# A three-layer fp32 kernel on one core: a later operand load, a second pair of split buffers, and a thinner schedule for unpacking weights

## Chip, cores and metric

One core of a Trainium2 chip. The metric is device microseconds (us) of one execution of the whole program, the median of several runs. Of the core's engines, TensorE (PE in the profile) does the matrix products, VectorE (DVE), ScalarE (ACT) and GpSimd (POOL) work element by element, and SyncE (SP) issues the DMAs, in order.

## What is computed

Windowed attention (two kinds of mask), then a mixture layer over 8 experts with weights `P` from a Sinkhorn loop, then a plain two-matrix layer with a squared ReLU:

```python
x = attention(q, k, v).reshape(2304, 512)
P = sinkhorn(x @ w_gate)                       # 2304 x 8
out = sum(P[:, e:e+1] * (relu(x @ w1[e]) @ w2[e]) for e in range(8))   # 512 -> 1024 -> 512
out = square(relu(out @ w_in)) @ w_out          # 512 -> 2048 -> 512
```

All of it is fp32. The last layer's weights `w_in` and `w_out` come as 64-bit numbers, which the kernel itself narrows to fp32.

## The kernel before

**Phases and steps.** After the attention the program runs 80 steps, in four phases: steps 0 to 31 and 32 to 63 are the expert layer for two sets of 1024 tokens ("pairs" of 512), steps 64 to 71 and 72 to 79 the last layer for the same two sets; `first` holds 0, 32, 64, 72. The remaining 256 tokens (the "single") go along in steps 0 to 31 and 64 to 71. One step handles 256 hidden features: a first product (units u1 to u7, a Strassen-like scheme of seven block products with matrices `blk` and `sum`), and the second product of the step before (l2 units, or v1 to v7 in the "mixed" phases 32 to 63 and 72 to 79). Each unit is mostly six 128x512 matmuls, since each fp32 operand is split into a high and a low part and three products are added. A step of the phase 32 to 63 has 14 units, one of the phase 64 to 71 has 18.

**What sets the order.** The order is written out: each engine's instructions stand in program order. `run(u)` issues a unit and then whatever `after(k, f)` put down k units later, so place k is the k-th unit of a step and what is past its end falls into the next step. Each engine runs its own list in order and waits only on semaphores, so that an instruction that waits holds up all behind it on its engine.

**What the change touches.**

- Splitting a weight or an operand into two parts is a cast on ACT (high) and a subtraction on DVE (low). `prep_w(i)` (L150) places the weight splits of a step; for steps 64 to 70 line 239 gives the places of `w2` high and low, the two POOL groups m3 and m4 (L229 to L234), and the "mix" high and low (L252). The last one's `mix_done` (L248) then issues the next load of `raw2` (L144) and the stores of the mix.
- `narrow` (L261) turns 64-bit weights into fp32 in 32 pieces of four stages: a load into `xb` (L266), two DVE stages of two instructions (L273 and L277; L281 and L284), and a last DVE stage of three (L288, L291, L295) with a store (L296). `narrow_on` (L1092) runs one stage, at places that `stages` (L1168 to L1172) gives: in steps 2 to 29 four a step, and in steps 52 to 60 two a step.
- `blocks_of(c, ...)` (L300) splits the seven blocks of a phase's activations, in halves j, for phase c + 1: a cast into `hi` (L307), a subtraction into `lo` (L310), stores of both to `b_dram` (L312), and a POOL subtraction for the next block (L303). There is one pair `hi`, `lo`. For c = 2 the pair is the two halves of `mixh0`, and `split_on(2, ...)` (L1162 to L1164) puts two splits in each of steps 66 to 69 and five in step 70, at places 2, 5, 8, 12 and 16.
- `operands_single` (L894) loads the single's activations from `y_dram` into an `xb` tile (L896) and splits them into `xs` (L339 on ACT, L340 on DVE), for use from step 64 on; it is called in step 60 (L1165).

`xb` tiles are two rotating buffers of 128x1024: a new tile gets the buffer of the tile before the last.

In u5, `after(0, ...)` copies the PSUM bank `pt` to SBUF (L717 on ACT), and only then may u6 write that bank; L713 is the same behind u4 and L701 behind u1. In the mixed phases v1 is copied from two banks to two others (L866 on ACT) before v2 adds to them; the same copies are behind casts (L646) whose input a POOL chain (L678) makes from the DVE product L667 (`mix<-s,pp`).

Of the kernel before, what the change touches and what calls it, by code (L numbers as in the profile page):

```python
# [1 line left out]

# [8 lines left out]
F32R = mybir.dt.float32r  # L11
# [24 lines left out]
NS1 = E * SPE  # L36
# [3 lines left out]
PAIRS = (0, 1280)  # L40
# [7 lines left out]
def tile_kernel(ctx: ExitStack, tc: tile.TileContext, a):  # L48
# [12 lines left out]
    at = att.enter_context(tc.tile_pool(name="at", bufs=2))  # L61
# [20 lines left out]
    y_dram = dram.tile([128, KC, NTOK], F32, name="y_dram")  # L82
# [13 lines left out]
    def tmp(name):  # L96
        return post[0].tile([128, 512], F32, tag="tmp", name=name, bufs=3)
# [8 lines left out]
    mixes = []  # L106
# [7 lines left out]
    def kept(i):  # L114
        return NS1 <= i < 2 * NS1 or i >= first[3]

    def mixed(i):
        return kept(i) and i < len(steps) - 1

    def place(i):  # L120
        return i % NS1 if i < first[2] else NS1 + (i - first[2]) % NS2

    def store(n, s, w):
        for h, z in zip("hl", w):
            nc.sync.dma_start(w_dram[n + h][s], z.bitcast(F32))

    def fetch(n, i, w):
        for h, z in zip("hl", w):
            nc.sync.dma_start(z.bitcast(F32), w_dram[n + h][place(i)])
# [7 lines left out]
    def load_w(i, which):  # L137
        if i >= len(steps) or kept(i):
            return
        moe, s = steps[i]  # L140
        while not moe and done[0] < 16 * s + 8 * which + 8:
            narrow_on()
        dst = raw1.rearrange("p b c -> p (b c)") if which == 0 else raw2
        nc.sync.dma_start(dst, src_w(i, which))  # L144
# [5 lines left out]
    def prep_w(i):  # L150
# [6 lines left out]
        def hi(w, src):  # L157
            return lambda: nc.scalar.copy(w[0], src)

        def lo(w, src, then=lambda: None):  # L160
            def f():
                nc.vector.tensor_tensor(out=w[1], in0=src, in1=w[0].bitcast(F32), op=ALU.subtract)  # L162
                then()

            return f

        n = i + 1
        late = 4 if i == 2 * NS1 else 0
# [3 lines left out]
        elif n < len(steps):  # L172
# [23 lines left out]
            at = (4, 5, 6, 8) if n == NS1 else (2, 3, 4, 5) if n == 1 else (2, 5, 10, 14) if n < NS1 else (2, 5, 8, 11)  # L196
            spread = n > first[2] + 1
            if spread:
                at = (6, 7, 14, 16)
# [6 lines left out]
        if kept(i):  # L206
            w2 = wset[i % 2]["w2"]
            out += [(0, lambda: fetch("w2", i, w2))]
            if mixed(i):
                out += [(0, lambda: fetch("mix", i, mixes[i % 2]))]  # L210
            if i == 2 * NS1 - 3:
                out += [(2, lambda: load_w(2 * NS1 + 1, 0)), (2, lambda: load_w(2 * NS1, 1))]
        elif i >= 0:
            w2 = wset[i % 2]["w2"]
            moe = i < NS1
            r = raw2.rearrange("p (f e d) -> p f e d", f=FC, e=2)
            z = mix32.rearrange("p (k d) -> p k d", k=4)

            def m1():
                tt(out=c(z, 0), in0=r[:, 0, 1], in1=r[:, 1, 1], op=ALU.add)  # L220
                tt(out=c(z, 2), in0=r[:, 0, 0], in1=r[:, 0, 1], op=ALU.subtract)

            def m2():
                tt(out=c(z, 1), in0=c(z, 0), in1=r[:, 0, 0], op=ALU.subtract)
                tt(out=c(z, 3), in0=r[:, 1, 0], in1=c(z, 1), op=ALU.subtract)
                load_w(i + 1, 1)

            def m3():
                tt(out=r[:, 1, 1], in0=r[:, 0, 1], in1=r[:, 1, 1], op=ALU.add)  # L229
                tt(out=r[:, 0, 1], in0=r[:, 0, 0], in1=r[:, 0, 1], op=ALU.subtract)  # L230

            def m4():
                tt(out=r[:, 0, 0], in0=r[:, 1, 1], in1=r[:, 0, 0], op=ALU.subtract)
                tt(out=r[:, 1, 0], in0=r[:, 1, 0], in1=r[:, 0, 0], op=ALU.subtract)  # L234

            if moe:
                at = (0, 0, 0, 1, 9, 10) if i == 0 else (1, 3, 6, 7, 13, 15)
            else:
                at = (11, 13, 14, 14, 16, 17) if late else (12, 13, 14, 14, 19, 20)
            if i:  # L240
                out += [(at[0], hi(w2, raw2)), (at[1], lo(w2, raw2, lambda: store("w2", place(i), w2)))]
            if moe:
                out += [(at[2], m1), (at[3], m2)]
                out += [(at[4], hi(mixes[1], mix32)), (at[5], lo(mixes[1], mix32, lambda: store("mix", place(i), mixes[1])))]
            elif i + 1 < first[3]:
                m = mixes[1]

                def mix_done():  # L248
                    load_w(i + 1, 1)
                    store("mix", place(i), m)  # L250

                out += [(at[2], m3), (at[3], m4), (at[4], hi(m, raw2)), (at[5], lo(m, raw2, mix_done))]  # L252
        else:
            w2 = wset[0]["w2"]
            out += [(6, hi(w2, raw2)), (7, lo(w2, raw2, lambda: kept_back.append(lambda: store("w2", 0, w2))))]
        return out

    def xb():
        return post[0].tile([128, 2 * T], F32, tag="xb", name="xb", bufs=2)
# [39 lines left out]

    def blocks_of(c, src, spaces):  # L300

        z11, z12, z21, z22, hi, lo = spaces
        sub = lambda o, x, y: nc.gpsimd.tensor_tensor(out=o, in0=x, in1=y, op=ALU.subtract)  # L303

        def block_of(k, j, z, then=lambda: None):
            def cast():
                nc.scalar.copy(hi, z)  # L307

            def rest():
                nc.vector.tensor_tensor(out=lo, in0=z, in1=hi.bitcast(F32), op=ALU.subtract)  # L310
                for h, y in enumerate((hi, lo)):
                    nc.sync.dma_start(b_dram[c][k, h, :, j], y.bitcast(F32))  # L312
                then()

            return cast, rest

        for j in range(2):
            def load(j=j):
                for h, zs in enumerate(((z11, z12), (z21, z22))):
                    for t, z in enumerate(zs):  # L320
                        nc.sync.dma_start(z, src[:, 2 * h + j, t * T:t * T + T])

            yield load, lambda: None
            yield block_of(0, j, z11, lambda: sub(z11, z12, z11))
            yield block_of(1, j, z21, lambda: sub(z12, z22, z12))
            yield block_of(4, j, z11, lambda: sub(z11, z22, z11))
            yield block_of(6, j, z12)
            yield block_of(2, j, z22, lambda: sub(z21, z21, z11))
            yield block_of(5, j, z11)
            yield block_of(3, j, z21)  # L330
# [217 lines left out]
    first = [0, NS1, 2 * NS1, 2 * NS1 + NS2]  # L548
# [24 lines left out]
    def after(k, f):  # L573

        due.setdefault(clock[0] + k, []).append(f)
# [318 lines left out]
    def operands_single():  # L894
        z = xb().rearrange("p (k n) -> p k n", n=NSG)
        nc.sync.dma_start(z, y_dram[:, :, SINGLE:SINGLE + NSG])  # L896
        return single_pieces(z)
# [3 lines left out]
    with tc.manual_schedule():  # L901
# [89 lines left out]
        def slot(i):  # L991
# [33 lines left out]
            (NG + LAG - 2, (f() for f in single_pieces(xf[:, :, SINGLE:SINGLE + NSG]))),  # L1025
        ]
        prep0 = [f for _, f in prep_w(-1)]
        for i in range(NG + LAG):
            slot(i)
# [27 lines left out]
        for g in gates:  # L1057
            for _ in g:
# [14 lines left out]
        two = lambda z: (z[:, :512], z[:, 512:])  # L1073
        held = [post[0].tile([128, T], F32, tag="pp", name="pp", bufs=3) for _ in range(3)]
        splits = [
            blocks_of(
                0, x_dram,
                (tmp("z11"), tmp("z12"), tmp("z21"), held[0], held[1].bitcast(F32R), held[2].bitcast(F32R)),
            ),
        ]  # L1080

        def split_on(c, k, k_lo):
            cast, rest = next(splits[c], (None, None))
            if cast:
                after(k, cast)
                after(k_lo, rest)
# [14 lines left out]
        for i in range(len(steps) + 1):  # L1101
# [52 lines left out]
                splits.append(blocks_of(1, y_dram[:, :, :2 * T], y0 + raw))  # L1154
            if i == 2 * NS1 + 1:
                y1 = two(mix32) + tuple(post[0].tile([128, T], F32, tag="pp", name="pp", bufs=3) for _ in range(2))
                splits.append(blocks_of(2, y_dram[:, :, PAIRS[1]:], y1 + two(mixes[0][0])))
            if SCALED <= i < NS1 - 2:
                split_on(0, 8, 9)
            elif NS1 + 4 <= i < 2 * NS1 - 4:  # L1160
# [1 line left out]
            elif 2 * NS1 < i < 2 * NS1 + 7:  # L1162
                for k in {2 * NS1 + 1: (3, 8, 16), 2 * NS1 + 6: (2, 5, 8, 12, 16)}.get(i, (3, 16)):
                    split_on(2, k, k + 1)  # L1164
            if i == first[2] - 4:  # L1165
                for k, f in enumerate(operands_single()):
                    after(8 + 2 * k, f)
            stages = {}  # L1168
            if SCALED - 1 <= i < NS1 - 2:
                stages = {2: 0, 16: 1, 17: 2, 1: 3}  # L1170
            elif 2 * NS1 - 12 <= i <= 2 * NS1 - 4:
                stages = {7: 1, 10: 2} if i % 2 else {7: 3, 8: 0}  # L1172
            for k, u in enumerate(order):
                run(u)
                if i < SCALED:
# [87 lines left out]
```

## Time and profile before

| | |
|---|---|
| median of 3 runs | 1961.62 us (1958.82 to 1964.09) |
| the profiled execution, its own time | 1961.02 us |
| its span, first to last instruction | 1959.2 us |
| mean granted TensorE clock | 0.994 |
| DMA moved | 491.84 MB, mean 251 GB/s |

"Busy" is the time in which an engine executes instructions. Matmuls overlap in the records, so the progress of PE is read from the starts of its matmuls. In rows of a timeline the bracket at the end is the idle time of the engine just before the row and what ended it; "PEclk" is the granted share of the full clock.

### The profile page before, as it was taken

The numbers are of one execution on the slowest core, as the hardware profiler recorded it, in microseconds if no ns is written. First come the engines' busy times: TensorE is split into PE (matmuls) and PEld (weight loads), VectorE is DVE, ScalarE is ACT, GpSimd is POOL, SyncE is SP. The second block draws the span as 40 slices with busy tenths as digits, with TensorE's granted clock in tenths as the row PEclk, the third lists the DMA queues.
The fourth block names the chain that finished last, engine by engine and source line by source line (L and its number), as shares of the span: only waits on it lengthen the run. The fifth ranks groups of instructions, "written<-read, shape, count | busy, mean of one in ns | idle before, by whom it ended". The sixth has DMA issues, their size and how long they took to land.

```text
span 1959.2 us, 29443 instructions
## 1 busy us (share of the span) xinstructions
PE 1926.5 (98%) x11050; PEld 1601.8 (82%) x11050; DVE 1630.2 (83%) x2337; ACT 747.3 (38%) x1238; POOL 633.5 (32%) x556
## 2 busy tenths in 40 slices
PE   8999999999999999999999999999998999999999
PEld 6778888888888888888888888888877878878887
DVE  5868888888888888887489998998998887775897
ACT  3544433333333332333333434333333354443443
POOL 4632333223333332222133424333232233330331
PEclk9999999999999999999999999999999999999999
DMA  7665667667666566666957758666575876669661
GB/s 261 217 239 197 253 262 269 259 257 265 236 251 234 229 241 247 230 232 263 395 216 273 285 215 297 252 252 249 225 260 193 311 293 252 251 241 392 232 253 67
DMA packets 166399, 491.84 MB, mean 251 GB/s; under 512 B 17248, under 2 KB 40176, under 8 KB 166256
## 3 DMA queue, kind: packets, MB, share of 16 engines
q1 hardware_dynamic: 166256, 489.96, 66.6%
q8 instruction: 87, 1.43, 0.3%
q14 instruction: 56, 0.46, 0.1%
HBM read 281.15 MB, written 208.74 MB: 250 GB/s over the span
## 4 chain that ended last, share of the span: by engine, by line
PE 89%; DVE 6%; DMA 1%; ACT 1%; POOL 1%; issue 1%; ACTq 0%; POOLq 0%; DVEq 0%
PE mm L779 28%; PE pt L566 15%; PE s L566 10%; PE xt L566 10%; PE mm L862 9%; PE mm L750 6%; PE s L862 3%; PE xt L862 3%; DVE acc L876 2%; PE xt L439 1%; DVE g L649 1%; PE mm L972 1%; PE s L387 1%; POOL r L678 1%; DMA sg<-w_mixl 1%
## 5 line engine op out<-in xcount | busy, mean ns | idle before, releaser
L779 PE MATMUL mm<-w2h,g 128*128 128x512 f32 x1312 | 406.5, 391 | 0.0
L801 DVE SCALAR_TENSOR_TENSOR acc<-mm,ptile,acc 128x512 f32<-128x512 f32 x290 | 216.7, 748 | 103.8 <-PE mm L779 103.5
L779 PEld LDWEIGHTS mm<-w2h,g 128*128 128x128 f32 x1312 | 245.5, 188 | 50.2
L779 PE MATMUL mm<-w2l,g 128*128 128x512 f32 x656 | 255.8, 390 | 0.0
L678 POOL TENSOR_TENSOR r<-mix,r 128x512 f32<-128x512 f32 x39 | 51.2, 1314 | 556.1 <-DVE mix L667 399.0
L649 DVE TENSOR_TENSOR g<-r,g 128x512 fp32r<-128x512 f32 x156 | 159.4, 1022 | 46.9 <-ACT g L646 45.2
L176 POOL TENSOR_TENSOR sums<-raw 128x256 f32<-128x256 f32 x40 | 32.7, 817 | 489.6 <-DVE suml L162 441.1
L646 ACT CAST g<-r 128x512 fp32r<-128x512 f32 x156 | 96.8, 621 | 137.4 <-PE mm L862 99.1
L779 PEld LDWEIGHTS mm<-w2l,g 128*128 128x128 f32 x656 | 123.4, 188 | 25.9
L876 DVE TENSOR_TENSOR acc<-mm,acc 128x512 f32<-128x512 f32 x226 | 144.6, 680 | 0.0
L566 PE MATMUL pt<-x_hi,sumh 128*128 128x512 f32 x320 | 124.9, 390 | 2.0 <-ACT s L713 2.0
L566 PE MATMUL s<-x_hi,blkh 128*128 128x512 f32 x320 | 125.4, 392 | 1.1 <-ACT pt L701 1.1
L566 PE MATMUL xt<-x_hi,sumh 128*128 128x512 f32 x320 | 124.7, 390 | 0.0
L566 PE MATMUL s<-x_lo,blkh 128*128 128x512 f32 x320 | 124.7, 390 | 0.0
L566 PE MATMUL s<-x_hi,blkl 128*128 128x512 f32 x320 | 124.6, 389 | 0.0
L566 PE MATMUL pt<-x_hi,suml 128*128 128x512 f32 x320 | 124.6, 389 | 0.0
L566 PE MATMUL xt<-x_hi,suml 128*128 128x512 f32 x320 | 124.5, 389 | 0.0
L566 PE MATMUL pt<-x_lo,sumh 128*128 128x512 f32 x320 | 124.5, 389 | 0.0
L566 PE MATMUL xt<-x_lo,sumh 128*128 128x512 f32 x320 | 124.5, 389 | 0.0
L604 ACT ACTIVATE sg<-mm 128x512 fp32r<-128x512 f32 (+1 forms) x35 | 19.7, 563 | 272.8 <-PE mm L750 272.8
L750 PE MATMUL mm<-xs,blkh 128*128 128x256 f32 x640 | 115.8, 280 | 0.0
L604 ACT ACTIVATE g<-s 128x512 fp32r<-128x512 f32 x96 | 59.6, 621 | 136.5 <-DVE s L718 69.0
(220 smaller groups left out, 4809.8 us busy)
## 6 DMA issues: line engine op xcount, KB each, us to landing
raw<-in_w SPq DMA_DIRECT2D x61, 512.0 KB, 6.5
blkh<-w_blkh SPq DMA_DIRECT2D x41, 512.0 KB, 3.6
blkl<-w_blkl SPq DMA_DIRECT2D x41, 512.0 KB, 4.4
sumh<-w_sumh SPq DMA_DIRECT2D x41, 512.0 KB, 5.3
suml<-w_suml SPq DMA_DIRECT2D x41, 512.0 KB, 6.1
w_blkh<-blkh SPq DMA_DIRECT2D x40, 512.0 KB, 6.1
w_blkl<-blkl SPq DMA_DIRECT2D x40, 512.0 KB, 6.5
w_sumh<-sumh SPq DMA_DIRECT2D x40, 512.0 KB, 6.3
```

The source lines that it names most:

```text
L176: tt(out=c(sums, 0), in0=c(raw1, 2), in1=c(raw1, 3), op=ALU.add)
L387: nc.tensor.matmul(ps[QB * head:QB * head + QB, 2 * (g % 3) + g // 3, :], qt[rows, pr, g * QB:g * QB + QB], kt[rows, pr, g * QB:g * QB + K ...
L566: nc.tensor.matmul(ps, w[:, c], z[:, x, j], start=start and k == 0, stop=stop and k == 5, skip_group_check=True)
L604: after(k, lambda: nc.scalar.activation(out=ghi, in_=src, func=AF.Relu))
L646: after(k, lambda: nc.scalar.copy(b[:, 0], src))
L649: lambda: nc.vector.tensor_tensor(out=b[:, 1], in0=src, in1=b[:, 0].bitcast(F32), op=ALU.subtract),
L678: sub = lambda o, x, y: nc.gpsimd.tensor_tensor(out=o, in0=x, in1=y, op=ALU.subtract)
L750: nc.tensor.matmul(ps[:, n * NSG:n * NSG + NSG], w[:, c], z[:, kc], start=k == 0, stop=k == 3 * KC - 1)
L779: nc.tensor.matmul(ps, g[:, c0 * 128:c0 * 128 + 128], wt[:, fc], start=k == 0, stop=k == 3 * FC - 1)
L801: nc.vector.scalar_tensor_tensor(out=dst, in0=ps, scalar=p, in1=dst, op0=ALU.mult, op1=ALU.add)
L862: nc.tensor.matmul(ps, w[wt][:, c], z[:, g], start=start and k == 0, stop=stop and k == 2, skip_group_check=True)
L876: nc.vector.tensor_tensor(out=o, in0=ps, in1=o, op=ALU.add)
```

## The change

It touches four places. In `prep_w` the mix split of step 64 moves from places 16 and 17 to 20 and 22, and in step 65 all six places move back by two. `blocks_of` takes any number of `hi`, `lo` pairs and uses them in turn; for c = 2 a second pair, the two halves of an `xb` tile taken in step 65, is added. `operands_single` is called in step 62 rather than 60. One more piece is narrowed in step 30 (load at place 2, stages at places 12, 13 and 14); the three pieces that are left run in steps 52 to 61, one stage a step, with the load of the next piece behind the last stage.

```diff
@@ -1,3 +1,4 @@
+import itertools
 from contextlib import ExitStack
 
 import numpy as np
@@ -236,7 +237,7 @@
             if moe:
                 at = (0, 0, 0, 1, 9, 10) if i == 0 else (1, 3, 6, 7, 13, 15)
             else:
-                at = (11, 13, 14, 14, 16, 17) if late else (12, 13, 14, 14, 19, 20)
+                at = (11, 13, 14, 14, 20, 22) if late else (14, 15, 16, 16, 21, 22) if n == first[2] + 2 else (12, 13, 14, 14, 19, 20)
             if i:
                 out += [(at[0], hi(w2, raw2)), (at[1], lo(w2, raw2, lambda: store("w2", place(i), w2)))]
             if moe:
@@ -299,10 +300,13 @@
 
     def blocks_of(c, src, spaces):
 
-        z11, z12, z21, z22, hi, lo = spaces
+        z11, z12, z21, z22 = spaces[:4]
+        pairs = itertools.cycle(zip(spaces[4::2], spaces[5::2]))
         sub = lambda o, x, y: nc.gpsimd.tensor_tensor(out=o, in0=x, in1=y, op=ALU.subtract)
 
         def block_of(k, j, z, then=lambda: None):
+            hi, lo = next(pairs)
+
             def cast():
                 nc.scalar.copy(hi, z)
 
@@ -1154,7 +1158,7 @@
                 splits.append(blocks_of(1, y_dram[:, :, :2 * T], y0 + raw))
             if i == 2 * NS1 + 1:
                 y1 = two(mix32) + tuple(post[0].tile([128, T], F32, tag="pp", name="pp", bufs=3) for _ in range(2))
-                splits.append(blocks_of(2, y_dram[:, :, PAIRS[1]:], y1 + two(mixes[0][0])))
+                splits.append(blocks_of(2, y_dram[:, :, PAIRS[1]:], y1 + two(mixes[0][0]) + two(xb().bitcast(F32R))))
             if SCALED <= i < NS1 - 2:
                 split_on(0, 8, 9)
             elif NS1 + 4 <= i < 2 * NS1 - 4:
@@ -1162,14 +1166,16 @@
             elif 2 * NS1 < i < 2 * NS1 + 7:
                 for k in {2 * NS1 + 1: (3, 8, 16), 2 * NS1 + 6: (2, 5, 8, 12, 16)}.get(i, (3, 16)):
                     split_on(2, k, k + 1)
-            if i == first[2] - 4:
+            if i == first[2] - 2:
                 for k, f in enumerate(operands_single()):
                     after(8 + 2 * k, f)
             stages = {}
             if SCALED - 1 <= i < NS1 - 2:
                 stages = {2: 0, 16: 1, 17: 2, 1: 3}
-            elif 2 * NS1 - 12 <= i <= 2 * NS1 - 4:
-                stages = {7: 1, 10: 2} if i % 2 else {7: 3, 8: 0}
+            elif i == NS1 - 2:
+                stages = {2: 0, 12: 1, 13: 2, 14: 3}
+            elif 2 * NS1 - 12 <= i <= 2 * NS1 - 3:
+                stages = ({8: 3, 9: 0}, {8: 1}, {8: 2})[(i - 2 * NS1 + 12) % 3]
             for k, u in enumerate(order):
                 run(u)
                 if i < SCALED:
```

The order of PE's instructions and of POOL's is the same in both kernels. The line numbers of the changed kernel are higher: by one up to `prep_w`, by four from the blocks' splits on.

**ACT, steps 60 and 62.** Rows of step 60, from the copy behind u4 to the first operands of the next unit; `xs<-xb` is the cast of the single's operands. Before:

```order
L713 COPY s_12973<-pt 128x512
L339 CAST xs<-xb 128x1024
L717 COPY s_12974<-pt 128x512
L646 CAST g_2263<-r_9039 128x512
L646 CAST g_2263<-mix_2266 128x512
```

Of the change, the same place in step 62:

```order
L717 COPY s_13249<-pt 128x512
L343 CAST xs<-xb 128x1024
L721 COPY s_13250<-pt 128x512
L650 CAST g_2263<-r_9050 128x512
L650 CAST g_2263<-mix_2266 128x512
```

In the change step 60 has the two copies next to each other, and the cast stands two steps later between the same two copies (L713 and L717 are L717 and L721 there).

**ACT, beginning of step 65.** `mixh<-raw` is the high half of step 64's mix, `s<-pt` the copies behind u4 and u5. Before:

```order
L701 COPY pt<-s 128x512
L158 CAST mixh_2268<-raw_109 128x1024
L611 ACTIVATE r<-s_13586 128x512
L611 ACTIVATE r<-s 128x512
L621 CAST g_2263<-g 128x512
L713 COPY s_13707<-pt 128x512
L621 CAST g_2264<-g 128x512
L717 COPY s_13708<-pt 128x512
```

Of the change:

```order
L705 COPY pt<-s 128x512
L615 ACTIVATE r<-s_13586 128x512
L615 ACTIVATE r<-s 128x512
L625 CAST g_2263<-g 128x512
L717 COPY s_13707<-pt 128x512
L625 CAST g_2264<-g 128x512
L159 CAST mixh_2268<-raw_109 128x1024
L721 COPY s_13708<-pt 128x512
```

The cast went from behind the copy of u1 to just ahead of the copy of u5; on DVE the low half moved with it, from ahead of the two products `g<-s,r` to behind the addition after u5.

**ACT, step 70.** The casts of blocks for c = 2 around the copies of u4 and u5. Before:

```order
L307 CAST mixh_2267<-mix_2266 128x512
L611 ACTIVATE r<-s 128x512
L713 COPY s_14825<-pt 128x512
L621 CAST g_2263<-g 128x512
L307 CAST mixh_2267<-mix_2266 128x512
L717 COPY s_14826<-pt 128x512
```

Of the change:

```order
L311 CAST xb<-mix_2266 128x512
L615 ACTIVATE r<-s 128x512
L717 COPY s_14826<-pt 128x512
L625 CAST g_2263<-g 128x512
L311 CAST mixh_2267<-mix_2266 128x512
L721 COPY s_14827<-pt 128x512
```

Nothing changed its place; successive casts write different pairs.

## Rows read from the trace of the kernel before

**Rows 1.** The page's busy time by engine (us, share of the span, instructions).

```profile
PE 1926.5 (98%) x11050; PEld 1601.8 (82%) x11050; DVE 1630.2 (83%) x2337; ACT 747.3 (38%) x1238; POOL 633.5 (32%) x556
```

**Rows 2.** Waits of PE over the span (total us, times, longest).

```profile
PE pt L566 <- ACT s L717: 10.1, 3, 6.0
```

**Rows 3.** Stretches: us; PE, PEld, DVE, ACT, POOL busy; PEclk; DMA share; GB/s.

```profile
880.00:920.00 40.00, 40.00 (x201) 34.09 (x200) 31.54 (x38) 12.92 (x19) 14.60 (x16) 1.00 0.61 228
1366.00:1492.00 126.00, 124.25 (x541) 100.64 (x540) 117.07 (x182) 45.80 (x80) 41.89 (x28) 1.00 0.59 218
1480.00:1520.00 40.00, 33.56 (x139) 26.99 (x138) 31.85 (x48) 13.64 (x23) 11.97 (x8) 0.91 0.55 211
1720.00:1760.00 40.00, 36.31 (x173) 30.53 (x172) 27.42 (x39) 16.41 (x26) 16.05 (x15) 0.91 0.63 238
1760.00:1800.00 40.00, 40.00 (x189) 33.62 (x188) 23.13 (x35) 10.88 (x18) 0.00 (x0) 1.00 1.01 393
```

**Rows 4.** Timeline of PE, steps 60, 65 and 70 (start, duration, instruction).

```profile
1497.07 0.39 PE L862 MATMUL xt<-g,mixl 128*128 128x512 f32 x1
1503.46 0.80 PE L566 MATMUL pt<-x_hi,blkh 128*128 128x512 f32 x1 [6.00 <-ACT s L717]
...
1508.16 0.39 PE L566 MATMUL xt<-x_hi,sumh 128*128 128x512 f32 x1
...
1601.20 0.50 PE L566 MATMUL pt<-x_hi,sumh 128*128 128x512 f32 x1 [1.48 <-ACT s L713]
...
1737.81 0.80 PE L566 MATMUL pt<-x_hi,blkh 128*128 128x512 f32 x1 [3.69 <-ACT s L717]
...
1743.05 0.39 PE L566 MATMUL xt<-x_hi,sumh 128*128 128x512 f32 x1
```

**Rows 5.** Timeline of ACT, steps 60, 65 and 70.

```profile
1501.88 1.04 ACT L339 CAST xs<-xb 128x1024 fp32r<-128x1024 f32 x1 [7.87 <-DMA xb<-y_dram]
...
1595.96 1.05 ACT L158 CAST mixh<-raw 128x1024 fp32r<-128x1024 f32 x1 [0.68 <-POOL raw L234]
...
1736.66 0.62 ACT L307 CAST mixh<-mix 128x512 fp32r<-128x512 f32 x1 [5.41 <-DMA b_dram<-mixh]
```

**Rows 6.** What SP waited for, steps 60 and 61.

```profile
SPq L896 <- DVE xb L295: 16.0, 1, 16.0
```

**Rows 7.** DMA issues: us to landing of the single's load; of `raw<-w`, steps 64 to 70.

```profile
xb<-y_dram SPq DMA_DIRECT2D x1, 512.0 KB, 4.0
...
DMA to landing us min/median/max: 3.6/4.5/5.8
```

**Rows 8.** Timeline of DVE, step 65.

```profile
1597.05 1.81 DVE L162 TENSOR_TENSOR mixl<-raw,mixh 128x1024 fp32r<-128x1024 f32 x1 [0.57 <-ACT mixh L158]
1598.79 2.02 DVE L615 SCALAR_TENSOR_TENSOR g<-s,r 128x512 f32<-128x512 f32 x2
```

**Rows 9.** Timeline of DVE, steps 59, 60 and 62 (the last without narrowing).

```profile
1476.21 0.41 DVE L273 TENSOR_SCALAR xb<-xb 128x512 int32<-128x512 int32 x1
1476.66 0.69 DVE L277 SCALAR_TENSOR_TENSOR xb<-xb 128x512 int32<-128x512 int32 x1
1477.27 0.68 DVE L718 TENSOR_TENSOR s<-xt,s 128x512 f32<-128x512 f32 x1
...
1484.33 0.68 DVE L667 SCALAR_TENSOR_TENSOR mix<-s,pp 128x512 f32<-128x512 f32 x1
...
1495.98 0.42 DVE L288 TENSOR_SCALAR xb<-xb 128x512 int32<-128x512 int32 x1
...
1497.15 0.69 DVE L295 TENSOR_TENSOR xb<-xb 128x512 f32<-128x512 f32 x1
...
1505.24 1.22 DVE L340 TENSOR_TENSOR xs<-xb,xs 128x1024 fp32r<-128x1024 f32 x1
...
1542.98 0.69 DVE L718 TENSOR_TENSOR s<-xt,s 128x512 f32<-128x512 f32 x1 [1.17 <-ACT s L717]
...
1549.01 0.68 DVE L667 SCALAR_TENSOR_TENSOR mix<-s,pp 128x512 f32<-128x512 f32 x1
```

**Rows 10.** Timeline of PE: v2 after a step with narrowing, and without.

```profile
1487.64 0.73 PE L862 MATMUL mm<-g,w2h 128*128 128x512 f32 x2 [0.44 <-ACT s L866]
...
1553.04 0.62 PE L862 MATMUL mm<-g,w2h 128*128 128x512 f32 x2
```

## The prediction, made before the changed kernel was run

> **What bounds the kernel now.** I read the page first: PE is busy 98% of the span, so the time is PE's stream of matmuls plus its holes [rows 1]. PE's order is the same in both kernels; the change can only close holes or open new ones. The view of waits names the largest: `pt` waiting for ACT's copy L717, 10.1 us in three waits [rows 2]. The table by stretches says where to look: PE busy 33.56 of 40 us around step 60 and 36.31 around step 70, both with a granted clock of 0.91, and 1.75 us idle in the stretch of steps 54 to 60 [rows 3]. The timelines then give each hole, and what ACT, DVE and SP did in it. A pair of matmuls takes 0.62 and one 0.39, so starts are 0.23 apart at full clock [rows 10].
>
> **Part 1: the single's load, step 60 to 62.** PE starts a matmul at 1497.07 and the next at 1503.46, 6.39 later: 6.16 lost [rows 4]. Behind it the granted clock is at its lower level, 1.2 GHz: the twelve matmuls from 1503.46 to 1508.16 take 4.70 instead of 12 x 0.23 = 2.76, another 1.94. The cause is in three views. ACT sat 7.87 before the cast L339, waiting for the DMA [rows 5]; L717, which frees u6's bank, stands behind it. SP had held that DMA back 16.0 for DVE's L295, the last stage of the last narrowed piece [rows 6], which ended at 1497.84 [rows 9]; the load then took 4.0 [rows 7]. So it is no slow load but one placed before its buffer is free. After the change the last piece ends at the same place of step 61 and the cast comes in step 62, at the place it had: about a step later, 14 units of six matmuls or 19 us, less some two units, against 4.0 for the load. ACT's cast does not depend on PE and can run in ACT's idle time ahead of u5's copy. **Gain 8.1.** On SP the load now stands behind the store of that piece and ahead of step 62's weight fetches; as the buffer is free by then, it delays them by one issue.
>
> The Trainium skill says the opposite of a later load: "DMA: Bandwidth & Descriptors", section "Rules for kernel authors", advises to issue a DMA early, compute, and wait for it late. By that rule the move is harmful, and the sum would keep these 8.1. Here the early place bought nothing, as the 16.0 on SP shows.
>
> **Part 2: narrowing, steps 52 to 61.** In a mixed step v2 starts at the earliest 2.63 after DVE's `mix<-s` ends (1485.01 to 1487.64); without narrowing the distance is 3.35 (1549.69 to 1553.04), so DVE may be 0.72 late at no cost [rows 9, 10]. It also has 1.17 idle before L718 [rows 9]. A two-instruction stage takes 1.06 (1476.21 to 1477.27), one of three 1.86 (1495.98 to 1497.84). Odd steps had two of the first kind, the second one behind L718, where no idle follows; even steps had the third behind the lateness of the odd ones. Seven holes result: 1.75 idle [rows 3], and each costs about 0.16 more between starts than the idle time shows (as 6.16 against 6.00) and 0.11 for a slow first matmul (0.73 against 0.62 [rows 10]): 3.6 in all. After it, a 1.06 alone fits into 1.17. The three steps with 1.86 (55, 58, 61) are late by 0.69, just under 0.72; if not, each costs what the even steps cost now, about 0.36, together 1.1. The move of L340 to step 62 adds 1.22 on DVE behind L718: 0.5 beyond the 0.72. **Gain 3.6 - 0.5 = 3.1, between 2.0 and 3.6.**
>
> **Part 3: one piece in step 30.** DVE gets 2 x 1.06 + 1.86 = 4.0 more within places 12 to 14, while 31.54 of 40 us there are busy and PE loses nothing [rows 3]. Accumulations wait behind it by up to 3 us, but three PSUM banks rotate and each unit has 1.4 us; by the end of step 30 DVE has caught up. A load of 512 KB and a store of 256 KB are added. **Cost 0, at most 1**; if the cover were gone, it would show as PE waiting for L801.
>
> **Part 4: the mix of step 64.** PE waits 1.48 for L713 at 1601.20; with the same 0.16 and 0.11 that is 1.7 [rows 4]. The chain: ACT's cast waits for POOL [rows 5], DVE's `mixl` waits for that cast and takes 1.81, the product L615 starts only at 1598.79, and ACT's cast L621 of it stands ahead of L713 [rows 8]. In the new order neither half of the mix stands ahead of these. The cast now precedes the copy of u5, but its input is ready and PE needs some 2 us to end u5. **Gain 1.7.** What is late next is the load of `raw2` behind `mixl`: about 6 us later, while the cast that reads it moves two units (2.8) back. A landing takes 3.6 to 5.8 [rows 7] and about 10 are left. The other small wait of step 65, u3 for L701, has nothing moved ahead of it and stays.
>
> **Part 5: two pairs for the blocks, steps 65 to 70.** At 1737.81 PE waited 3.69, so 3.85 between starts, and the twelve matmuls to 1743.05 took 5.24 instead of 2.76: 6.3 in all [rows 4]. ACT had waited 5.41 in the block's cast L307 for the stores of the block three places before [rows 5], with L717 behind it. With pairs in turn this cast writes the pair that was stored in step 69. The cast three places later (place 8) now meets the pair whose stores landed at 1736.6; without the hole ACT comes to it at about 1736, so it may wait half a microsecond, and no copy that PE needs is near behind it. **Gain 6.3.**
>
> **The sum.** 8.1 + 3.1 + 1.7 + 6.3 = 19.2. The profiled execution took 1961.0 (the median of the runs, 1961.62, is 0.6 above): 1961.0 - 19.2 = 1941.8, so **1942**. Bounds: with 1.1 more in part 2 and 1 in part 3, 1944; with 0.5 more gained in part 2, 1941.3.
>
> **The rivals.**
>
> *The load is late after all* (the rule above): if SP reached it late and ACT waited in step 62 as in step 60, the 8.1 come back: 1950. For it: the same in-order queue. Against: the 16.0 are DVE's, and DVE's part is over a step earlier. 6%.
>
> *The stores become the bound*, or the second pair does not do what it says: in step 71 DMA is at 1.01 with 393 GB/s [rows 3], and step 70 loses 6.3 us in which the queue could drain. If the fetches of step 71 then end later, PE stops at step 72 for what part 5 gained: 1948. Against: around step 70 only 238 GB/s moved, and the same bytes in 6.3 us less are below 300. 12%.
>
> *Slower.* In steps 65 and 66 ACT's `w2` cast waits for `raw2`; ACT is in order, the accumulation copies stand behind it, PE runs out of banks, and the lower clock follows as in step 60. It decides from a landing of about 10 us; to end slower the two holes must cost 19.2 + 5.9, which takes landings over 20: 1967 or more. Nothing in [rows 7] comes near: 2%.
>
> *Several at once*, with the holes of parts 1 and 5 both back under another name, gives 1956, no difference that can be told: 4%.
>
> *More than forecast*, the wait of u3 going too, gives about 1940: 4%.
>
> **Chances.** The forecast has 72%, from 1940 to 1945. About 0.3% or 5.9 us is what a measurement can tell from no change. Faster by more than that: forecast, late load, stores and the better case, 72 + 6 + 12 + 4 = 94%. Same: 4%. Slower: 2%. The range for 8 in 10 takes the forecast, the better case, most of the stores' case, and some 2.5 us for the spread of the runs around their median: 1937.5 to 1949.
>
> **What would show it.** Right: ACT's L343 (the old L339) in step 62 without a wait on a DMA; granted clock 1.00 in all stretches from step 32 to 71; the wait of `pt` on the copy L721 (old L717) down from 10.1 to under 1; the holes before v2 in steps 54 to 60 gone, one of about half a microsecond in step 63; in step 70 no cast L311 waiting over 1 us. Wrong: a wait of ACT for `raw` or `y_dram`, PE waiting at the beginning of step 72 for `x_hi` or `x_lo`, or a stretch with a clock under 1 that was not there before.

## The result and the profile after

| | before | changed |
|---|---|---|
| median | 1962.86 us (1958.82 to 1965.59, 6 runs) | 1943.69 us (1940.42 to 1949.17, 6 runs) |
| ratio to before, 95% interval | | 0.9907 (0.9888 to 0.9925) |
| profiled execution, its own time | 1961.02 us | 1944.46 us |

The forecast was 1942, in a range of 1937.5 to 1949, and faster. The page of the changed kernel, against [rows 1]:

```profile
PE 1921.6 (99%) x11050; PEld 1601.8 (82%) x11050; DVE 1627.4 (84%) x2337; ACT 747.0 (38%) x1238; POOL 636.5 (33%) x556
```

Waits of PE over the span (total us, times, longest), the one that answers to [rows 2] and one that is new:

```profile
PE pt L570 <- ACT s L721: 0.4, 1, 0.4
...
PE mm L866 <- DMA w2l<-w_w2l: 0.4, 1, 0.4
```

The 10.1 us behind L717 (now L721) are 0.4. The table by stretches (us; PE, PEld, DVE, ACT, POOL busy; PEclk; DMA share; GB/s), against [rows 3]:

```profile
1366.00:1480.00 114.00, 114.00 (x504) 94.40 (x503) 106.26 (x164) 41.15 (x72) 35.93 (x24) 1.00 0.67 240
1480.00:1520.00 40.00, 40.00 (x179) 33.13 (x178) 37.44 (x58) 14.92 (x26) 11.98 (x8) 1.00 0.73 271
...
1720.00:1760.00 40.00, 40.00 (x189) 33.64 (x188) 31.27 (x46) 19.73 (x31) 8.97 (x8) 1.00 0.88 337
```

PE is busy throughout, at the full clock, where the kernel before lost 1.75 us, 6.4 us and 3.7 us in the stretches that answer to these three. ACT's timeline around the cast of the single's operands in step 62 and around a block's cast in step 70 (two pieces of one view), against [rows 5]:

```profile
1530.40 0.59 ACT L717 COPY s<-pt 128x512 f32<-128x512 f32 x1 [0.94 <-PE pt L570]
1530.88 1.05 ACT L343 CAST xs<-xb 128x1024 fp32r<-128x1024 f32 x1
1533.12 0.59 ACT L721 COPY s<-pt 128x512 f32<-128x512 f32 x1 [1.19 <-PE pt L570]
...
1721.04 0.62 ACT L311 CAST mixh<-mix 128x512 fp32r<-128x512 f32 x1
1722.69 0.59 ACT L721 COPY s<-pt 128x512 f32<-128x512 f32 x1 [1.03 <-PE pt L570]
```

Neither cast waits any more (7.87 and 5.41 before); the copy behind it waits for PE, as it should.

**Where the time went, stretch by stretch.** DVE's addition L718 (L722 in the changed kernel) runs once a step, behind u6. Its start is a mark in each step that all kernels share. Timeline of DVE of the kernel before, steps 8, 30, 36, 63, 67 and 79:

```profile
325.00 0.67 DVE L718 TENSOR_TENSOR s<-xt,s 128x512 f32<-128x512 f32 x1
...
896.17 0.68 DVE L718 TENSOR_TENSOR s<-xt,s 128x512 f32<-128x512 f32 x1
...
1035.98 0.69 DVE L718 TENSOR_TENSOR s<-xt,s 128x512 f32<-128x512 f32 x1 [1.17 <-ACT s L717]
...
1560.66 0.69 DVE L718 TENSOR_TENSOR s<-xt,s 128x512 f32<-128x512 f32 x1 [1.00 <-ACT s L717]
...
1656.83 0.68 DVE L718 TENSOR_TENSOR s<-xt,s 128x512 f32<-128x512 f32 x1
...
1932.46 0.69 DVE L718 TENSOR_TENSOR s<-xt,s 128x512 f32<-128x512 f32 x1 [0.32 <-ACT s L717]
```

The same of the changed kernel:

```profile
327.41 0.68 DVE L722 TENSOR_TENSOR s<-xt,s 128x512 f32<-128x512 f32 x1
...
898.53 0.69 DVE L722 TENSOR_TENSOR s<-xt,s 128x512 f32<-128x512 f32 x1
...
1038.63 0.69 DVE L722 TENSOR_TENSOR s<-xt,s 128x512 f32<-128x512 f32 x1 [1.17 <-ACT s L721]
...
1551.99 0.69 DVE L722 TENSOR_TENSOR s<-xt,s 128x512 f32<-128x512 f32 x1 [0.58 <-ACT s L721]
...
1646.71 0.68 DVE L722 TENSOR_TENSOR s<-xt,s 128x512 f32<-128x512 f32 x1
...
1915.96 0.69 DVE L722 TENSOR_TENSOR s<-xt,s 128x512 f32<-128x512 f32 x1 [0.32 <-ACT s L721]
```

Differences of neighbouring marks give a table, and the same marks were read in the profile of every experiment. "To 8" is the time from the start of the span to step 8, in which the program is the same in all kernels.

| us | to 8 | 8 to 30 | 30 to 36 | 36 to 63 | 63 to 67 | 67 to 79 |
|---|---|---|---|---|---|---|
| before | 325.00 | 571.17 | 139.81 | 524.68 | 96.17 | 275.63 |
| changed | 327.41 | 571.12 | 140.10 | 513.36 | 94.72 | 269.25 |
| difference | +2.41 | -0.05 | +0.29 | -11.32 | -1.45 | -6.38 |
| a1_single_only | 322.31 | 571.13 | 139.82 | 517.46 | 96.15 | 274.75 |
| a2_free_buffer | 330.82 | 571.13 | 139.81 | 518.00 | 96.15 | 274.65 |
| a3_old_narrowing | 321.24 | 571.13 | 139.82 | 517.42 | 94.70 | 269.25 |
| a4_one_pair | 327.20 | 571.17 | 139.98 | 513.29 | 94.67 | 274.72 |
| b1_one_pair_spread | 321.10 | 571.17 | 141.37 | 513.32 | 94.75 | 269.25 |
| b2_old_mix | 329.02 | 571.17 | 141.07 | 513.29 | 96.20 | 269.27 |
| c1_later_w2 | 325.22 | 571.13 | 141.27 | 512.77 | 93.49 | 269.25 |
| d2_piece_in_20 | 327.09 | 571.82 | 139.84 | 513.28 | 94.73 | 269.26 |
| d1_both | 325.75 | 571.48 | 139.82 | 512.72 | 93.55 | 269.25 |
| after_again | 327.76 | 571.13 | 141.66 | 513.29 | 94.73 | 269.26 |

The columns behind step 36 repeat to about 0.1 us wherever the code there is the same, with one exception (67 to 79 of the kernel before, see the last section). That is far better than single runs of one kernel, which spread over up to 9 us (1940.42 to 1949.17). So small effects are read from these columns, and the medians only say which kernel is faster as a whole. The difference in the table adds up to -16.50, which is that of the two spans (1959.2 and 1942.7).

### The profile page after: what moved, and what is told of

It reads as the page before. It is cut to its first block, busy times and chain, and to the rows that moved or that the text cites. A ratio compares the mean times of both kernels' runs of the same rounds, so it can differ in the third digit from the quotient of the medians.

```text
span 1942.7 us, 29441 instructions
## 1 busy us (share of the span) xinstructions
PE 1921.6 (99%) x11050; PEld 1601.8 (82%) x11050; DVE 1627.4 (84%) x2337; ACT 747.0 (38%) x1238; POOL 636.5 (33%) x556
## 4 chain that ended last, share of the span: by engine, by line
PE 94%; DVE 4%; issue 1%; ACT 1%; DMA 0%; POOL 0%; SPq 0%; DVEq 0%; ACTq 0%; POOLq 0%
PE mm L783 28%; PE pt L570 16%; PE s L570 11%; PE xt L570 11%; PE mm L866 10%; PE mm L754 6%; PE s L866 4%; PE xt L866 4%; PE xt L443 1%; PE mm L976 1%; PE s L391 1%; DVE acc L880 1%; PE pt L428 1%; DMA w2l<-w_w2l 0%; PE mm L477 0%
```

## The experiments

**a1_single_only**, on the kernel before:

```diff
-            if i == first[2] - 4:
+            if i == first[2] - 2:
```

> The kernel before with one edit: the single's operands are loaded in step 62. Theory (the hole of step 60 was a load behind a buffer that was not free): the hole of 6.2 us and its 1.9 us at the lower clock go, 8.1 us in all; the median 1962.9 falls to about 1954.8. ACT's cast L339 stands in step 62 and waits for no DMA; the granted clock around step 60 is 1.00; the holes before v2 in steps 54 to 60 (1.75 us idle) and in step 70 (3.69) stay. Rival (the load is slow or late wherever it stands): the cast waits about 7 us in step 62 and the time stays at 1962.9.

Measured: median 1953.29 us (six runs), ratio to before 0.9949 (0.9933 to 0.9966). Between steps 36 and 63 it is 7.22 us faster; the other 0.88 of the 8.1 stands between steps 67 and 79, where it changes nothing (below, on the lower clock). The cast in step 62 has no idle time before it (timeline of ACT), so the rival, a load that waits anywhere, falls:

```profile
1529.60 1.05 ACT L339 CAST xs<-xb 128x1024 fp32r<-128x1024 f32 x1
```

PE's timeline shows why the gain is not 8.1 in its own place, at the beginnings of steps 61 and 63, each with the matmul before it (start, duration, instruction):

```profile
1503.82 0.39 PE L566 MATMUL xt<-x_hi,suml 128*128 128x512 f32 x1
1504.30 0.73 PE L862 MATMUL mm<-g,w2h 128*128 128x512 f32 x2
...
1542.29 0.39 PE L566 MATMUL xt<-x_hi,suml 128*128 128x512 f32 x1
1542.90 0.74 PE L862 MATMUL mm<-g,w2h 128*128 128x512 f32 x2 [0.23 <-ACT s L866]
```

The first starts 0.48 after its predecessor instead of 0.23. With the slow first pair behind it that is an eighth hole of narrowing, 0.36 in all, which the big hole of step 60 had swallowed. The second is what the moved L340 costs, 0.61 between starts, 0.5 in all. 8.1 - 0.36 - 0.5 = 7.2.

**a2_free_buffer**, on the kernel before:

```diff
-        z = xb().rearrange("p (k n) -> p k n", n=NSG)
+        z = raw1.rearrange("p b c -> p (b c)").rearrange("p (k n) -> p k n", n=NSG)
```

> The kernel before with one edit: the single's load stays in step 60, but goes into raw1, which nothing uses then, in place of an xb tile. Theory (the buffer was the cause, not the place): SP does not hold the load for DVE's L295 any more, it lands before step 60's cast, and the same 8.1 us go as by the later load: about 1954.8, with a wait of `pt` on L717 of about 4 us in place of 10.1. Rival (the place is too early for another reason, such as SP's queue or the place of the cast on ACT): ACT still waits several us in step 60, and the time is within 2 us of 1962.9.

Measured: median 1956.26 us (six runs), ratio 0.9961 (0.9949 to 0.9973). SP's queue in step 60 (timeline):

```profile
1487.60 0.60 SPq L896 DMA_DIRECT2D raw<-y_dram  x1
```

and ACT's timeline:

```profile
1499.63 1.05 ACT L339 CAST xs<-raw 128x1024 fp32r<-128x1024 f32 x1
```

SP issues the load 4.6 us behind step 59's mark, where it was 20.6 in the kernel before: 16 us earlier, though it stands at the same place in the program. The cast has no idle time before it. 36 to 63 is 6.68 us faster. So the buffer was the cause. That it gains 0.54 less than the later load has its reason on DVE, which now has the last narrowing stage and L340 in one step; PE waits 1.2 us at the beginning of step 61 (timeline of PE):

```profile
1513.93 0.73 PE L862 MATMUL mm<-g,w2h 128*128 128x512 f32 x2 [1.22 <-ACT s L866]
```

The rule that the prediction set against this step (the Trainium skill, "DMA: Bandwidth & Descriptors", section "Rules for kernel authors": issue a DMA early, compute, and wait late) thus agrees with this run, where an early load has a free destination, and did not apply to the kernel before, where the early load stood in the queue for 16.0 us [rows 6].

**a3_old_narrowing**, on the changed kernel:

```diff
-            elif i == NS1 - 2:
-                stages = {2: 0, 12: 1, 13: 2, 14: 3}
-            elif 2 * NS1 - 12 <= i <= 2 * NS1 - 3:
-                stages = ({8: 3, 9: 0}, {8: 1}, {8: 2})[(i - 2 * NS1 + 12) % 3]
+            elif 2 * NS1 - 12 <= i <= 2 * NS1 - 4:
+                stages = {7: 1, 10: 2} if i % 2 else {7: 3, 8: 0}
```

> The changed kernel with the old narrowing (no piece in step 30, two stages a step in steps 52 to 60). Theory: seven holes before v2 return in steps 54 to 60, about 1.75 us idle and 3.6 us between starts, and the small gap near 970 us (w2l, 0.77) falls to about 0.3: 1943.7 + 3.1 = 1946.8. Rival (narrowing cost nothing, the holes fill elsewhere): within 0.5 us of the changed kernel in the profile from step 32 to the end. The median cannot tell 3 us apart; the gaps between PE's starts decide.

Measured: median 1943.02 us (four runs), ratio 0.9901 (0.9877 to 0.9924), which cannot be told from the changed kernel. By the marks it is 4.06 us slower from 36 to 63 and 0.28 faster from 30 to 36. Eight matmuls before v2 start late again, of which the timeline of PE shows the seventh and the last, this one with the matmul before it:

```profile
1483.79 0.73 PE L866 MATMUL mm<-g,w2h 128*128 128x512 f32 x2 [0.43 <-ACT s L870]
...
1502.74 0.39 PE L570 MATMUL xt<-x_hi,suml 128*128 128x512 f32 x1
1503.21 0.73 PE L866 MATMUL mm<-g,w2h 128*128 128x512 f32 x2
```

The theory holds, and the eighth hole is the one that a1_single_only showed: 3.6 for seven and 0.36 for it are the 4.0. Its profiled span is 1940.3 us all the same, 2.4 less than that of the changed kernel, since up to step 8 it took 6.2 less.

**a4_one_pair**, on the changed kernel:

```diff
-...blocks_of(2, y_dram[:, :, PAIRS[1]:], y1 + two(mixes[0][0]) + two(xb().bitcast(F32R))))
+...blocks_of(2, y_dram[:, :, PAIRS[1]:], y1 + two(mixes[0][0])))
```

> The changed kernel with a single pair of buffers for the blocks of the third phase. Theory: step 70's cast L311 waits again about 5.4 us for the stores, PE stops 3.7 us before u6 and runs at the lower clock behind it: 6.3 us more, about 1950.0. Rival (step 71's full DMA takes the time in either case, so that the pair only moves it): the hole returns, but step 72 starts at the same time, and the kernel takes 1943.7.

Measured: median 1952.03 us (four runs), ratio 0.9943 (0.9922 to 0.9963). ACT's timeline in step 70:

```profile
1726.03 0.62 ACT L311 CAST mixh<-mix 128x512 fp32r<-128x512 f32 x1 [5.31 <-DMA b_dram<-mixh]
```

Behind it PE waits for L721, and twelve matmuls further on it starts the second row (timeline of PE):

```profile
1727.18 0.50 PE L570 MATMUL pt<-x_hi,blkh 128*128 128x512 f32 x1 [3.59 <-ACT s L721]
...
1731.63 0.39 PE L570 MATMUL xt<-x_hi,sumh 128*128 128x512 f32 x1
```

The stretch around it and the next (columns as above):

```profile
1710.00:1750.00 40.00, 36.41 (x177) 30.60 (x176) 28.31 (x39) 17.11 (x27) 15.60 (x14) 0.96 0.65 248
1750.00:1790.00 40.00, 40.00 (x190) 33.60 (x189) 22.29 (x34) 10.75 (x18) 0.00 (x0) 1.00 1.01 394
```

The wait is back, 5.31 for 5.41, and 67 to 79 is 5.47 us longer, where 6.3 was expected; the last section says where the rest is. Step 71 with its full DMA (1.01) is as it was, with PE busy 40.00 of 40: the rival, that step 71 takes the gain back, falls.

**b1_one_pair_spread** takes the single pair of a4_one_pair and spreads the pieces:

```diff
-{2 * NS1 + 1: (3, 8, 16), 2 * NS1 + 6: (2, 5, 8, 12, 16)}.get(i, (3, 16))
+{2 * NS1 + 5: (3, 16), 2 * NS1 + 6: (3, 16)}.get(i, (3, 10, 16))
```

> The changed kernel with a single pair again, but the sixteen pieces of the blocks' list laid out as three in each of steps 65 to 68 (places 3, 10, 16) and two in steps 69 and 70, where five stood in step 70. Theory (a pair cannot be written again until its two stores have landed, some 5 to 9 us, and step 70's places were 4 us apart): with at least 5 units (7 us) between casts most of step 70's wait goes without the second pair. Counted from the same early step to the last one, the kernel is within 1 us of the changed one, and any cast L311 that waits costs PE under 1 us. Rival (the second pair itself is what helps, and a single one waits at any place): holes of 2 to 4 us appear in steps 65 to 69, and the kernel is 3 us or more slower than the changed one.

Measured: median 1942.87 us (four runs), ratio 0.9899 (0.9882 to 0.9916). From 36 to 79 it takes 877.32 us, the changed kernel 877.33. ACT waits once for the stores, in step 66 (waits of ACT, steps 65 to 70), and PE does not wait for it; PE's only wait in these steps is that of u3 in step 65, 1.1 us, which the changed kernel has too:

```profile
ACT mixh L311 <- DMA b_dram<-mixh: 2.2, 1, 2.2
```

So the second pair is one cure and the spacing another; the cause is five splits in one step on one pair.

**b2_old_mix**, on the changed kernel:

```diff
-                at = (11, 13, 14, 14, 20, 22) if late else (14, 15, 16, 16, 21, 22) if n == first[2] + 2 else (12, 13, 14, 14, 19, 20)
+                at = (11, 13, 14, 14, 16, 17) if late else (12, 13, 14, 14, 19, 20)
```

> The changed kernel with the old places of the mix of step 64 and of step 65's splits. Theory: PE waits 1.5 us for the copy L717 in step 65 again, 1.86 between starts, and the small wait of the changed kernel in step 66 (0.36 between starts) goes: 1.6 us more from an early step to the last one. Rival (another wait in steps 65 to 67 takes its place, so the new places only move it): under 0.5 us of difference there. The medians cannot tell either.

Measured: median 1945.86 us (four runs), ratio 0.9913 (0.9895 to 0.9930). 63 to 67 takes 1.48 us more, and PE waits as in [rows 4] (its timeline, step 65):

```profile
1595.13 0.50 PE L570 MATMUL pt<-x_hi,sumh 128*128 128x512 f32 x1 [1.48 <-ACT s L717]
```

**c1_later_w2**, on the changed kernel:

```diff
-                at = (11, 13, 14, 14, 20, 22) if late else ...
+                at = (11, 17, 18, 18, 21, 23) if late else ...
@@
-                    after(8 + 2 * k, f)
+                    after(6 + 2 * k, f)
```

> The changed kernel with two more moves: the single's cast and subtraction at places 6 and 8 of step 62 in place of 8 and 10, and in step 64 the subtraction of w2's low part four places later (17, with m3 and m4 at 18, the mix at 21 and 23). Theory (both remaining holes are DVE work ahead of something PE waits for): the hole before v2 in step 63 (0.62 between starts) and the one before u3 in step 65 (1.53) close, about 1.9 us less from an early step to the last one. Rival (the later mix makes ACT wait for POOL ahead of the copies, or raw2 lands late for step 65's w2): a new hole of 1 us or more in steps 65 or 66, and nothing gained. By the median 1943.7 falls to about 1941.8 at best.

Measured: median 1942.71 us (four runs), ratio 0.9896 (0.9880 to 0.9911). 36 to 63 is 0.59 us shorter and 63 to 67 1.23, 1.82 together as expected: the hole before v2 in step 63 and the one before u3 in step 65 are gone. But steps 30 to 36 took 1.17 us more than in the changed kernel's profile, with the same code there. Whether that is the cost of step 30's piece is what the next run asks.

**d2_piece_in_20**, on the changed kernel:

```diff
                 stages = {2: 0, 16: 1, 17: 2, 1: 3}
+                if i == 20:
+                    stages = {2: 0, 6: 1, 7: 2, 10: 3, 11: 0, 16: 1, 17: 2, 1: 3}
-            elif i == NS1 - 2:
-                stages = {2: 0, 12: 1, 13: 2, 14: 3}
```

> The changed kernel with the extra narrowed piece in step 20 in place of step 30 (load at place 2, stages at 6, 7 and 10, the next load at 11). Theory (step 30's piece puts its 768 KB ahead of steps 31 to 33, where the DMA engines are busy all the time, so that w2l comes late in step 32 or 33): no wait for w2l<-w_w2l, and from step 30 to step 36 the 139.8 us of the kernels without that piece in place of 140.0 to 141.4. Step 20 to step 24 takes as long as before (102.1 to 103.9 us by four steps), since PE waits for nothing there. Rival (the lost time of steps 32 and 33 comes from DVE or varies by itself): 139.8 is exceeded by 0.2 to 1.6 us here too.

Measured: median 1945.24 us (four runs), ratio 0.9917 (0.9901 to 0.9934). Steps 30 to 36 take 139.84 us again and no wait for w2l is left. So the time does not vary by itself: the piece costs it. The run moves the piece's DVE work out of step 30 together with its bytes, so it does not say which of the two counts (below, part 3). One clause of the theory falls: 8 to 30 takes 0.70 us more, because PE waits in step 20 for an accumulation on DVE, the sign that the prediction had named for step 30 (L801 there; waits of PE, 630 to 745 us):

```profile
PE mm L783 <- DVE acc L805: 0.4, 1, 0.4
```

**d1_both** joins the edits of c1_later_w2 and d2_piece_in_20.

> The same with the two moves of the run c1_later_w2 besides. Theory: the gains add, 1.8 us behind step 36 and what d2_piece_in_20 gains ahead of it: from step 8 to step 79 about 1586.5 us (the changed kernel 1588.6, the kernel before 1607.5), all of it at the full clock. Rival: as for the two runs. The median should be 1940 to 1942, below both kernels, with the start of the program varying by more than the gain.

Measured: median 1942.58 us (four runs), ratio 0.9902 (0.9887 to 0.9917). From step 8 to 79 it takes 1586.82 us, expected 1586.5, against 1588.55 of the changed kernel. By the trace it is the shortest of all behind step 8, 1.7 us below the changed kernel and 1.1 below c1_later_w2. The medians, 1942.58 and 1943.69 with intervals that overlap, do not show it, and 1942.58 is above the 1940 to 1942 expected.

**after_again** is the changed kernel itself.

> The changed kernel once more, unchanged, for two spreads. Theory (what differed from the forecast lies ahead of step 8): from step 36 to step 79 it takes 877.3 us again within 0.2; up to step 8 anything from 321 to 331 us, the more the longer the granted clock was at its lower level there; from step 30 to 36 between 139.8 and 141.4. Rival (the execution shown was unlucky behind step 36 too): 877.3 changes by 1 us or more.

Measured: median 1943.67 us (four runs), ratio 0.9908 (0.9892 to 0.9924). 36 to 79 takes 877.28 us (877.33 in the first profile), so the time there repeats. 30 to 36 takes 141.66, a little more than the 141.4 expected at most. Waits of PE from 935 to 985 us:

```profile
PE mm L866 <- ACT pt L705: 0.7, 1, 0.7
PE mm L866 <- DMA w2l<-w_w2l: 0.5, 1, 0.5
PE xt L570 <- DMA suml<-w_suml: 0.3, 1, 0.3
```

## Why the prediction was right, and where it was not

**Parts 1 and 2, the single's load and the narrowing: 11.2 forecast, 11.32 measured** (36 to 63). The split between them depends on what is undone first: 7.22 for the load alone on the kernel before, 4.06 for the narrowing on top of it. The prediction had booked the 0.5 for L340 under part 2, and it counted seven holes where the eighth lay under the hole of part 1. In the changed kernel the 0.5 shows as forecast, 0.62 between starts and a slow first pair; of the three steps with the three-instruction stage none lost anything. The 1.94 at the lower clock, a term of part 1, stands in one profile alone, the only one with that hole, and how far it repeats is not shown. PE's timeline at the beginning of step 63:

```profile
1543.57 0.39 PE L570 MATMUL xt<-x_hi,suml 128*128 128x512 f32 x1
1544.19 0.73 PE L866 MATMUL mm<-g,w2h 128*128 128x512 f32 x2 [0.23 <-ACT s L870]
```

**Part 3, the piece in step 30: forecast 0, at most 1; measured 0.29 in the execution shown.** This is the step that failed. In the six profiles of kernels with that piece, steps 30 to 36 take 139.98 to 141.66 us, in the six without it 139.81 to 139.84: 0.15 to 1.85 us, 1.1 on the mean, and more than the bound of 1 in four of the six. The prediction weighed DVE's busy share and the PSUM banks, named L801 as the sign, and passed over the load and the store with a sentence. What PE waits for in step 32 is `w2l`, which SP fetches late, and SP's lateness begins in step 30. The stretch some 8 to 16 us behind that step's mark, in the kernel before and in the changed one (columns as above):

```profile
904.00:912.00 8.00, 8.00 (x49) 7.09 (x48) 5.97 (x8) 0.28 (x1) 3.81 (x4) 1.00 0.44 180
906.50:914.50 8.00, 8.00 (x48) 7.11 (x47) 7.86 (x12) 0.42 (x1) 2.70 (x3) 1.00 0.26 107
```

DVE is now busy 7.86 of 8 us. PE loses nothing by that (step 30 takes 25.69 us in both kernels), but SP does, since its stores stand behind DVE's work (waits of SP, 897 to 925 us):

```profile
SPq L126 <- DVE xb L289: 10.3, 1, 10.3
SPq L297 <- DVE xb L296: 2.2, 1, 2.2
```

The first was 8.1 in the kernel before, for the same store of `suml`; the second is the piece's own store. Behind the step's mark `suml` is stored at 13.2 instead of 11.8 us and the next weights, `mixh`, at 16.2 instead of 12.2. So the DMA engines move 107 GB/s in this stretch where they moved 180, and from some 20 us behind the mark on they are nearly full up to step 32 (changed kernel):

```profile
940.00:960.00 20.00, 20.00 (x103) 16.41 (x102) 6.85 (x10) 6.41 (x11) 0.00 (x0) 1.00 1.05 395
960.00:980.00 20.00, 19.63 (x92) 15.81 (x91) 11.76 (x17) 11.51 (x21) 5.99 (x4) 1.00 1.04 380
```

SP stays some 2 us late through them. It issues step 32's w2l 1.72 us ahead of that step's mark where d2_piece_in_20 issues it 3.65 ahead (961.84 and 963.56; 960.30 and 963.95), 1.9 later. SP's row of the changed kernel:

```profile
961.84 0.74 SPq L130 DMA_DIRECT2D w2l<-w_w2l  x1
```

and of d2_piece_in_20:

```profile
960.30 0.61 SPq L130 DMA_DIRECT2D w2l<-w_w2l  x1
```

In the six profiles with the piece this fetch is issued 62.7 to 64.1 us behind step 30's mark, in the six without it 60.4 to 61.4. That the piece is the cause is shown. How it delays SP is read from the traces and no run separates it: the 768 KB more would be 2.0 us at 390 GB/s, which fits in size, but between the piece's load and its store the engines were far from full (0.26), so SP's wait for DVE has the better case.

**Part 4, the mix: 1.7 forecast, 1.45 measured** (63 to 67). The 1.48 of L713 is gone; what is left over is a new small wait in step 66, 0.36 between starts instead of 0.23 and a slow first matmul, 0.24 in all, which the prediction did not have (timeline of PE):

```profile
1616.67 0.39 PE L783 MATMUL mm<-w2l,g 128*128 128x512 f32 x1
1617.03 0.50 PE L570 MATMUL pt<-x_hi,sumh 128*128 128x512 f32 x1
```

**Part 5, the two pairs: 6.3 forecast, 6.38 measured** (67 to 79). Step 70's casts wait for no store. The half microsecond for place 8 did not come. That the size agrees so closely is in part luck: 6.3 and 6.38 come from the same profile of the kernel before, and the three other profiles with the old pair and places (a1_single_only, a2_free_buffer, a4_one_pair) lie only 5.4 to 5.5 above the changed kernel.

**Its signs.** The five that were to show it right are all there: L343 without a wait on a DMA, the clock at 1.00 (as the mean from the mark of step 32 to that of step 71, and in the stretches above), `pt` waiting 0.4 for L721, one hole before v2 in step 63 and no other, and step 70's casts without a wait. Of the rivals none took place: the load came in time, step 72 started as before (35.50 us from the mark of step 71 to that of 72 in both kernels), and ACT never waited for raw2.

**The sum.** Behind step 36 the change gives 11.32 + 1.45 + 6.38 = 19.15 us, forecast 19.2. That the profiled executions differ by only 16.6 comes from 0.29 in part 3 and from 2.41 ahead of step 8, which no part of the change touches. The medians differ by 19.2 as forecast, and that they do so to a tenth is luck: from step 8 to step 79 the changed kernel's first profile is 18.9 below the kernel before, its second (after_again) 17.4. The forecast time itself is 1.7 too low, since it was counted from the profiled execution, 1961.0, while the median of the kernel before is 1962.86.

## What to carry over

Ask of a late load what its place in the queue waited for before asking for more bandwidth or an earlier place: here the destination was not free, and a later load and a free buffer cured it alike. When a piece of work moves to another step, ask which stores and loads stand behind it in the queue, and not only which matmuls do. Here they went out late, and stretches with full DMA engines kept the delay of 2 us for some 40 us. Where the start of a program varies by more than the effect, a mark that stands once a step in all kernels measures tenths of a microsecond in single profiles, where medians cannot; where a hole lowers the clock behind it, even these marks differed by 0.9 us between profiles.

## What was not expected of the hardware

**The start varies by 9.7 us, and the granted clock goes along with it.** Up to step 8 the program is the same in all kernels, yet it takes 321.10 to 330.82 us. The first 110 us in a3_old_narrowing (321.24; columns as above):

```profile
0.00:110.00 110.00, 101.62 (x2560) 81.22 (x2561) 74.77 (x150) 48.98 (x124) 58.91 (x66) 1.00 0.72 236
```

and in a2_free_buffer (330.82):

```profile
0.00:110.00 110.00, 100.99 (x2467) 81.36 (x2468) 71.84 (x146) 46.12 (x119) 58.85 (x66) 0.91 0.67 213
```

PE has idle time there in each (8 to 9 of 110 us), and in one execution its clock stays at the higher level while in the other it spends some 20 of the 110 us at the lower (an estimate from the mean of 0.91: 2 x 0.09 x 110). Over all twelve profiles the two shortest starts (321.10 and 321.24) have 1.00 there, the two longest (329.02 and 330.82) 0.92 and 0.91. Why the executions differ was not tried.

**The same hole costs more or less by the clock behind it.** Step 70's hole was 3.7 us idle in the kernel before and 3.6 in a4_one_pair, but 40 us around it have a mean clock of 0.91 in the first [rows 3] and of 0.96 in the second; the stretch 67 to 79 is 6.38 and 5.47 us longer than in the changed kernel. The twelve matmuls behind the hole took 5.24 us in the first [rows 4] and 4.45 in the second (1727.18 to 1731.63), where twelve at the full clock take 2.76. a1_single_only and a2_free_buffer, with the old single pair, also stand 0.88 and 0.98 below the kernel before there. So 0.9 us of a1_single_only's gain is of this kind and not the edit's.
